# A fused attention and long-convolution kernel: the inverse transform's first stage in pairs, f32 products of q and k in the front, phases two at once, and a new order

## The chip, the core and the metric

The kernel runs on one core of a Trainium2 chip. A core has a matrix engine (PE), a vector engine (DVE), a scalar engine (ACT), a general engine (POOL) and an engine that issues most DMAs (SP). PE reads SBUF and writes PSUM; ACT and DVE read PSUM and write SBUF. Each engine executes its own instructions in the order in which the program lists them, so that an instruction that must wait holds up all that stand behind it on its engine.

The metric is the time of one execution on the device, in microseconds. Times of several executions are told by their median.

## What is computed

Two independent blocks, whose results stand side by side in the output (2048 rows, 576 + 576 columns):

```python
def _A_ref(x, wqkv, wo):               # x: 1 x 2048 x 576, 32 heads of 18, window 256
    q, k, v = ...                       # (x @ wqkv), by heads
    scores = einsum("bhqd,bhkd->bhqk", q, k) * 18 ** -0.5
    scores = where(0 <= i - j < 256, scores, -1e9)
    return (softmax(scores) @ v) @ wo

def _B_ref(u, A, B, C, log_dt, Dskip): # u: 1 x 2048 x 576, 128 states to a channel
    dt = exp(log_dt)
    K = einsum("dn,dnl,dn->dl", C, exp(dt * A * l), dt * B).real
    y = irfft(rfft(pad(u)) * rfft(pad(K)))[:2048]
    return y + u * Dskip
```

Block A is attention in a sliding window of 256 rows. Block B is a convolution of each channel with its own filter K of 2048 taps; K must first be built from 128 complex exponentials to a channel.

## The kernel before

**Stages.** `build` runs four stages in a row, "front", "tables", "first" and "rest". Each stage is a set of streams (generators), and a string in `PLAN` gives the order of their steps by hand: a letter alone is the next step of a stream, a letter with a digit is the oldest piece of later work of that kind (`post`) which a step of this stream has left behind, such as the copy of a product out of PSUM. The instructions are issued in the order of the strings, and each engine takes its own from it. `SLOTS` says which of three PSUM buffers ("ring", two banks each) the next product takes. Two more PSUM buffers ("pp") belong to the projection, later one ("po") to the attention's output.

**Front** (streams A, B: parameters; C: scales; V: v of the first rows; P: projection). x and the weights are loaded. x @ wqkv is made in f16 at the accuracy of f32: each operand is scaled by a power of two and split in a high and a low f16 part, and a product is 14 matmuls (`mm14`, L205: high x high, low x high, high x low over 576 = 4 x 128 + 64 rows, the last rows of both parts put together). The scales need the largest absolute value of all of x and of all weights (`scales`, L193, DVE), taken over the partitions on POOL (L180). `xconv` and `wconv` make the parts. `proj` then makes q and k in nine products of 128 x 512 for each chunk c of 512 rows, and v in eight products of 128 x 288. ACT copies a q/k product as f16 (`qk_hi`, L451), DVE makes the low part (L454), and SP stores both. While the scales aren't known yet, `vfirst` makes v of the first chunk with f32 matmuls from the raw x and weights (L399, L404), eight products of 288 columns.

**Tables** (G, N, R, M, X: the filter K; U: first stage of u's transform; P goes on; Z, s: first steps of the attention). The filter is built in 18 steps q of 32 channels, and half of a step, 16 channels, is c = 2q or 2q + 1. `t_phase` (one for each c) makes phases on PE (512 columns), `fold` takes off their whole turns (an ACT copy to integers at L512, a DVE subtraction at L515), `t_sin` turns them to sines and cosines (ACT, L556 to L558, once for each c), `t_q` multiplies with magnitudes (DVE, L603 to L606), `t_prod` and `t_add` make the other factor (POOL L588, DVE L594), `t_taps` makes 64 matmuls of taps (L617), and `t_dft` the filter's first transform stage. The tile fr, which holds phases and then sines, has FR = 5 buffers of one half each. `s1_u` does the first transform stage of u in 16 steps: it loads ut, multiplies (L494), ACT and DVE copy one half each to ust (L499), and SP stores ust to gx in DRAM. ut and ust have two buffers each (pool s1u).

**Rest** (s, a, v, n: attention; k, c, d, f, e: convolution; l, y, w: output projection). The attention works in 16 items: maxima of scores (L908, L916, DVE L942), scores and exponentials (L984, L997, ACT L1002), products with v (L1022), normalisation. The convolution goes through 24 steps n: `conv_load` loads xk from gx and gk, `spectra` (stream c) makes the second stage of both transforms with 32 matrix products of 64 x 32 tiles (L720, 384 columns) into two ring slots, ACT copies them to X (L728), DVE and POOL multiply the spectra to Y (L736 to L743), and `inverse` (stream d, L754) does the first stage of the inverse transform: 16 matmuls of 32 x 64 tiles over 192 columns. The four groups of 32 rows (b) write to one of the two halves of the PSUM partitions each, 64 (b mod 2), and bank b div 2 of one ring slot. ACT copies the slot to ho (L761), and two DMAs store it to h. `hload` and `clast` do the second stage of the inverse (L817), and `wo` multiplies the attention's output with wo (L205 again).

A matmul of f32 operands shows as two records in the profile.

## Time and profile before

| | us |
|---|---|
| median of the three runs | 777.35 |
| lowest and highest of them | 774.3, 778.51 |
| the profiled execution | 772.85 |
| its span, first to last instruction | 771.1 |

The profile is of one execution. Its page gives the busy time of each engine (PEld is PE's loading of weights, which overlaps with PE), the chain of work that ended last, followed back from the last instruction to what released it, and the costliest groups of instructions by line. In a group's row stand the line, the engine, the operation, what it writes and reads with the shapes, and the count, then the busy time in us and the mean of one in ns, and last the engine's idle time ahead of them with what ended it. In a row of the timeline or the chain the first number is the start and the second the duration, both in us. In a row of the busy times by stage each engine's busy time is followed by its number of instructions. The granted TensorE clock of the whole span is 0.98 of full speed.

| engine | busy us | share of the span |
|---|---|---|
| PE | 686.8 | 89% |
| PEld | 403.5 | 52% |
| DVE | 538.7 | 70% |
| ACT | 548.3 | 71% |
| POOL | 415.8 | 54% |

### The profile page before, as it was taken

To read this page: it belongs to the slowest core of one execution; us is meant where nothing else is said; L and a number is where in the kernel's file an instruction comes from. 1 tells how busy PE (TensorE), PEld (TensorE's weight loads), DVE (VectorE), ACT (ScalarE), POOL (GpSimd) and SP (SyncE) were. 2 spreads that over 40 slices of the span, in tenths; PEclk is the share of its full clock that TensorE was granted. 3 is DMA by queue.
4 is the path that set the end of the run, shared out by engine and by line. 5 is a ranking of instruction groups with operands and counts; after the bars stand their busy time and mean duration, and the time that the engine had idled before them with its cause. 6 is when DMAs were issued, how large, how long until landed. Compare 5 with 4: busy or idle time off the path is not lost.

```text
span 771.1 us, 29480 instructions
## 1 busy us (share of the span) xinstructions
PE 686.8 (89%) x12956; PEld 403.5 (52%) x12956; DVE 538.7 (70%) x689; ACT 548.3 (71%) x755; POOL 415.8 (54%) x309
## 2 busy tenths in 40 slices
PE   3768768999999989999888998989899989999997
PEld 2523334556655655566445545545554545576675
DVE  5884888677787677888859877988886788631200
ACT  2267986888988878895467686677687687766722
POOL 2242886888788696867016553544255355354420
PEclk9978999999999999999989999999999999999999
DMA  8996342863657686757967667586588766767875
GB/s 308 345 248 151 86 109 56 196 156 97 133 146 201 145 195 188 178 150 155 244 213 236 201 186 246 176 273 183 177 246 233 231 206 191 230 189 250 251 237 174
DMA packets 215904, 150.67 MB, mean 195 GB/s; under 512 B 103530, under 2 KB 195818, under 8 KB 215520
## 3 DMA queue, kind: packets, MB, share of 16 engines
q1 hardware_dynamic: 214160, 146.28, 67.0%
q0 software_dynamic: 1616, 2.52, 1.1%
q8 instruction: 101, 1.65, 0.9%
q14 instruction: 27, 0.22, 0.1%
HBM read 83.50 MB, written 65.11 MB: 193 GB/s over the span
## 4 chain that ended last, share of the span: by engine, by line
PE 53%; DVE 12%; ACT 12%; issue 4%; DMA 4%; SPq 2%; POOL 0%; ACTq 0%; DVEq 0%
PE pp L205 9%; PE po L1022 9%; PE ring L205 7%; DVE m L942 5%; PE ring L908 4%; PE ring L754 4%; PE ring L984 4%; PE ring L720 3%; PE ring L617 2%; PE ring L817 2%; PE ring L494 2%; ACT P L1002 2%; PE ring L506 2%; DMA K<-kz 2%; PE ring L633 1%
## 5 line engine op out<-in xcount | busy, mean ns | idle before, releaser
L942 DVE TENSOR_REDUCE m<-ring 128x2 f32<-128x640 f32 (+4 forms) x256 | 188.3, 778 | 42.4 <-PE ring L916 37.1
L588 POOL TENSOR_TENSOR m<-A,tr 128x1024 f32<-128x1024 f32 x72 | 142.0, 1991 | 43.1 <-DVE m L594 37.1
L1002 ACT ACTIVATE P<-ring,esc 128x1024 f32<-128x1024 f32 (+2 forms) x86 | 88.4, 1060 | 28.7 <-PE ring L997 28.0
L1002 ACT ACTIVATE raw<-ring,esc 128x1024 f32<-128x1024 f32 (+2 forms) x74 | 76.9, 1061 | 28.6 <-PE ring L997 26.7
L736 POOL TENSOR_TENSOR t<-X 128x768 f32<-128x768 f32 x24 | 45.9, 1913 | 79.7 <-ACT X L728 79.5
L1065 POOL TENSOR_TENSOR oh<-osb,oh 128x1024 f16<-128x1024 f32 x16 | 35.4, 2211 | 66.2 <-ACT oh L1061 63.3
L205 PE MATMUL pp<-xh,wh 128*128 128x512 f16 x180 | 47.3, 393 | 14.5 <-ACT vst L406 6.4
L205 PEld LDWEIGHTS <-wh 128*128 128x128 f16 x324 | 31.2, 100 | 49.6 <-issue 10.5
L916 PE MATMUL ring<-sm,idb 64*64 64x128 bf16 x896 | 52.8, 219 | 0.0
L603 DVE TENSOR_TENSOR Q<-fr,ring 128x1024 f32<-128x1024 f32 x36 | 43.8, 1216 | 11.6 <-ACT ring L527 11.3
L728 ACT ACTIVATE X<-ring 128x768 f32<-128x768 f32 x48 | 36.7, 811 | 21.2 <-PE ring L720 12.5
L594 DVE TENSOR_TENSOR m<-m,m 128x1024 f32<-128x1024 f32 x36 | 48.3, 1342 | 4.2 <-POOL m L588 4.2
L1057 POOL TENSOR_TENSOR osb<-osb,T 128x1024 f32<-128x1024 f32 x16 | 37.8, 2365 | 24.3 <-DVE T L1052 21.8
L205 PE MATMUL pp<-xh,wl 128*128 128x512 f16 x180 | 48.5, 403 | 1.5 <-DVE wl L373 1.5
L908 PE MATMUL ring<-K,raw 54*64 54x320 f16 (+4 forms) x576 | 43.3, 308 | 5.6 <-DVE m L942 1.6
L569 POOL TENSOR_TENSOR tr<-tr,mab 128x768 f32<-128x768 f32 x18 | 33.7, 1871 | 25.6 <-ACT tr L564 25.6
L908 PEld LDWEIGHTS <-raw 54*64 54x64 f16 x704 | 26.1, 104 | 39.3 <-issue 35.6
L742 POOL TENSOR_TENSOR Y<-t,t 128x384 f32<-128x384 f32 x24 | 24.0, 1000 | 39.7 <-DVE t L736 18.7
L720 PE MATMUL ring<-xk,w 64*32 64x384 f32 x768 | 41.5, 491 | 3.5 <-issue 2.8
L997 PE MATMUL ring<-tm,idb 64*64 64x256 bf16 (+2 forms) x640 | 44.6, 257 | 0.0
L984 PEld LDWEIGHTS <-K 55*64 55x64 f16 x1280 | 29.1, 106 | 27.8 <-issue 24.0
L617 PE MATMUL ring<-Q,m 128*32 128x64 f32 x2304 | 39.2, 220 | 4.1 <-DVE m L594 2.0
(170 smaller groups left out, 1668.5 us busy)
## 6 DMA issues: line engine op xcount, KB each, us to landing
gx<-ust SPq DMA_DIRECT2D x16, 576.0 KB
gk<-kst SPq DMA_DIRECT2D x36, 256.0 KB
xk<-gx SPq DMA_DIRECT2D x24, 384.0 KB
xk<-gk SPq DMA_DIRECT2D x24, 384.0 KB
h<-ho SPq DMA_DIRECT2D x48, 192.0 KB
hp<-h SPq DMA_DIRECT2D x24, 384.0 KB
K<-kz SPq DMA_DIRECT2D x14, 512.0 KB
raw<-qz SPq DMA_DIRECT2D x11, 512.0 KB
```

The lines of the kernel that those rows point to most:

```text
L205: self.nc.tensor.matmul(ps, u, v, start=(i == 0), stop=(i == len(ops) - 1))
L588: tt(m[part], A[:, ch, a0:a0 + 8].unsqueeze(3).to_broadcast(sh), tr[:, ch, part, 0:8].unsqueeze(2).to_broadcast(sh), op=OP.mult)
L594: self.nc.vector.tensor_tensor(m[0], m[0], m[1], op=OP.add)
L617: nc.tensor.matmul(kp[32 * st:32 * st + 32, j, :], m[:, ch, 32 * term:32 * term + 32], Q[:, ch, term, :], start=(term == 0), stop=(term == ...
L720: nc.tensor.matmul(pi[i][32 * b:32 * b + 32, s, :384], self.w2[64 * r:64 * r + 64, t, o:o + 32], x[64 * r:64 * r + 64, 2 * s + q].rearrang ...
L736: mul(ts[i], X[:, :, :, :192].rearrange("p i s j -> p s i j"), X[:, i, :, 192:].unsqueeze(2).to_broadcast(sh), op=OP.mult)
L908: nc.tensor.matmul(ps[z:z + 64, b, :n], d["Q"][rr, 2 * b + pp, 64 * qb:64 * qb + 64], d["K"][rr, 2 * b + pp, k0:k1], start=True, stop=Fals ...
L916: nc.tensor.matmul(out, self.idb[rr], self.sm[rr], start=False, stop=True, skip_group_check=True)
L942: self.nc.vector.tensor_reduce(out, x, axis=AX.X, op=OP.max)
L984: nc.tensor.matmul(ps[z:z + 64, b, off:off + w], d["K"][rr, 2 * b + pp, kc:kc + 64], d["Q"][rr, 2 * b + pp, q0:q0 + w], start=(k == 0), st ...
L1002: nc.scalar.activation(P[:, :, lo:hi], ps[:, :, lo:hi], AF.Exp, scale=self.esc)
L1022: nc.tensor.matmul(po[32 * p:32 * p + 32, z, q0:q0 + w], V[64 * z:64 * z + 64, kb * 76 + 19 * p:kb * 76 + 19 * p + 32], P[p % 2][64 * z:64 ...
```

## The change

There are six parts.

1. `inverse` takes two steps n and n + 1 at once, into two ring slots. Their matmuls alternate, and step n + 1 writes to the other half of the PSUM partitions, so that the four row groups and both halves are in use in turn. The order of the rows in the constant `i1` and the place of `spectra`'s output are exchanged for odd steps, so that Y lies where the second step needs it. There are 12 such pieces.
2. `spectra` is cut in two steps, one ring slot each. X and its products get two buffers (pool fy), Y three (fy2).
3. `t_phase`, `fold` and the sines work on both halves of a step q at once (1024 columns). FR is 3, with buffers of twice the size.
4. In the front, `vfirst` gives way to `qk_first`: q and k products m = 0 to 5 of the first chunk are made with f32 matmuls of 256 columns from raw x and weights, in three ring slots with two products each, and scaled when they are copied out (`qsc`). v of the first chunk is made by `proj` like the others. The weights of v get a scale of their own (`vscale`, with a maximum on ACT), their block is loaded last, and the parts of x and of the weights are made in separate steps, the low ones posted for later.
5. ust has a pool of its own (s1o) with one buffer; ut keeps two.
6. The four strings of `PLAN` and `SLOTS` are new. In "front" there are 13 steps of P ahead of the tables instead of 11 products' thirds and one empty step, in "tables" 27 copies of q/k products instead of 33 and 32 copies of v instead of 24.

The core of the diff:

```diff
-        i1[b ^ s, :, t, s, 0] = np.concatenate([co.T, -si.T], 1)
-        i1[b ^ s, :, t, s, 1] = np.concatenate([si.T, co.T], 1)
+        i1[b ^ s ^ t % 2, :, t, s, 0] = np.concatenate([co.T, -si.T], 1)
+        i1[b ^ s ^ t % 2, :, t, s, 1] = np.concatenate([si.T, co.T], 1)
...
     def inverse(self, n):
-        nc, (ch, t), Y = self.nc, divmod(n, 8), self.Y.pop(n)
-        ps = self.slot()
+        pr = [(k, self.Y.pop(n + k), self.slot()) for k in range(2)]
         for s in range(2):
             for i in range(2):
                 for b in range(4):
-                    o = (2 * s + i) * 64
-                    nc.tensor.matmul(ps[64 * (b % 2):64 * (b % 2) + 64, b // 2, 192 * s:192 * s + 192],
-                                     self.i1[32 * b:32 * b + 32, t, o:o + 64], Y[32 * b:32 * b + 32, i, s],
-                                     start=(s == 0 and i == 0), stop=(i == 1), skip_group_check=True)
+                    for k, Y, ps in pr:
+                        o, z = (2 * s + i) * 64, 64 * (b % 2 ^ k)
+                        self.nc.tensor.matmul(ps[z:z + 64, b // 2, 192 * s:192 * s + 192],
+                                              self.i1[32 * b:32 * b + 32, n % 8 + k, o:o + 64], Y[32 * b:32 * b + 32, i, s],
+                                              start=(s == 0 and i == 0), stop=(i == 1), skip_group_check=True)
+        for k, Y, ps in pr:
+            self.post("1", (ps,), lambda n=n + k, ps=ps: self.h_out(n, ps))
...
-    def spectra(self, n):
+    def spectra(self, n, i):
...
+        for q in range(2):
+            for s in range(2):
+                for r in range(2):
+                    b = 2 * q + (r ^ s ^ n % 2)
...
-    def t_phase(self, c):
-        x = self.slot()[:, 0]
-        self.outer(x, self.ps, c // 2, [self.mul["c_ct"]], c % 2 * HC, HC)
+    def t_phase(self, q):
+        x = self.slot()
+        for e in range(2):
+            self.outer(x[:, e], self.ps, q, [self.mul["c_ct"]], e * HC, HC)
...
-        for c in (2 * q, 2 * q + 1):
-            f = self.fr[c]
-            nc.scalar.activation(f[:, 1], f[:, 0], AF.Abs)
...
+        f = self.fr[q]
+        nc.scalar.activation(f[:, 1], f[:, 0], AF.Abs)
...
+    def qk_first(self):
+        nc, w, x = self.nc, self.wt, self.xt
+        for g in range(NF // 2):
+            ps = None
+            for h in range(2):
+                cs = slice(256 * g + 128 * h, 256 * g + 128 * h + 128)
+                for hf in range(2):
+                    yield "PE", (w, x[hf]), *(("ring",) if ps is None else ())
+                    self.hold = ps = self.slot() if ps is None else ps
+                    for k in range(4):
+                        nc.tensor.matmul(ps[:, h, 256 * hf:256 * hf + 256], w[:, k, cs], x[hf][:, k], start=(k + hf == 0),
+                                         stop=False, skip_group_check=True)
             yield "PE", ()
             for hf in range(2):
+                for h in range(2):
+                    r, cs = slice(64 * h, 64 * h + 64), slice(256 * g + 128 * h, 256 * g + 128 * h + 128)
+                    nc.tensor.matmul(ps[:, h, 256 * hf:256 * hf + 256], w[r, 4, cs], x[hf][r, 4], start=False, stop=True,
+                                     skip_group_check=True)
...
+    def vscale(self):
+        nc, sp = self.nc, self.p["const"]
+        yield "Activation", (self.wt,)
+        nc.scalar.activation(self.wl[:, :, 1152:1728], self.wt[:, :, 1152:1728], AF.Abs, accum_out=self.amx[:, 10:11])
...
-            st = self.p["s1u"].tile([128, 2, D], F32, name="ust")
+            st = self.p["s1o"].tile([128, 2, D], F32, name="ust")
...
-        w(2)
+        w(0)
         x(0)
         x(1)
-        w(0)
         w(1)
         for c in range(2, 8):
             x(c)
+        w(2)
...
-            self.FR = 5
+            self.FR = 3
...
-            for n, b in (("cc", 1), ("fs", 2), ("fy", 1), ("wo", 1), ("wo2", 1), ("wor", 2), ("wy", 2)):
+            for n, b in (("cc", 1), ("fs", 2), ("fy2", 3), ("fy", 2), ("wo", 1), ("wo2", 1), ("wor", 2), ("wy", 2)):
```

The part of the new order of "tables" that holds steps 1 and 2 of u's transform (U is a step, U1 and U2 are the two copies to ust, U4 is its store):

```
U4UUP4U1U2U4P1PP2RXX5X
```

More of the change, by code (lines that the diff above doesn't have):

```diff
@@ L28 @@
 NQ = 18
+NF = 6
 GC = 4 * JJ
@@ L144 @@
+    "201210212020"
 )
@@ L401, in vfirst @@
             yield "PE", ()
             for hf in range(2):
-                r = slice(64 * hf, 64 * hf + 64)
-                nc.tensor.matmul(ps[hf], x[r, 4, ts], w[r, 4, 1152 + 288 * hf:1440 + 288 * hf], start=False, stop=True)
-            for hf in range(2):
-                self.post("1", (ps[hf],), lambda v=v, hf=hf, x=ps[hf]: nc.scalar.activation(
-                    v[:, 16 * hf:16 * hf + 16, 0:18], x.rearrange("p (h d) -> p h d", d=18), AF.Copy))
-        yield "SP", (), lambda: self.known and not self.pend.get("V1")
@@ L429, in proj @@
                 self.post("1", (ps,), lambda c=c, m=m, ps=ps: self.qk_hi(c, m, ps))
-            for tk in range(4 if c else 0):
+            for tk in range(4):
                 v = self.vst[tk]
@@ L495, in s1_u, with store @@
                                      ut[ch][64 * r:64 * r + 64, 288 * k:288 * k + 288], start=True, stop=True)
-            end = self.both("4", (st,), lambda ch=ch, st=st: nc.sync.dma_start(gv[:, ch:32:16], st))
+            def store(ch=ch, st=st):
+                nc.sync.dma_start(gv[:, ch:32:16], st)
+                self.n["u"] += 1
+            end = self.both("4", (st,), store)
             def evac(op, r, st=st, ps=ps, end=end):
@@ L723, in spectra @@
         sh = [128, 2, 2, 192]
         def first():
-            X = fy.tile([128, 2, 2, 384], F32, name="X")
-            for i in range(2):
-                nc.scalar.activation(X[:, i], pi[i][:, :, :384], AF.Copy)
-            ts = [None, None]
-            end = self.each(lambda: self.post("3", (), lambda: third(*ts)))
-            self.post("2", (X,), lambda: second(X, 0, tt, ts, end))
-            self.post("6", (X,), lambda: second(X, 1, nc.gpsimd.tensor_tensor, ts, end))
+            if i == 0:
+                self.X[n] = fy.tile([128, 2, 2, 384], F32, name="X")
@@ L734, in second @@
+            X = self.X[n]
+            nc.scalar.activation(X[:, i], pi[:, :, :384], AF.Copy)
+            if i:
+                del self.X[n]
+                ts = [None, None]
+                end = self.each(lambda: self.post("3", (), lambda: third(*ts)))
+                self.post("2", (X,), lambda: second(X, 0, tt, ts, end))
+                self.post("6", (X,), lambda: second(X, 1, nc.gpsimd.tensor_tensor, ts, end))
         def second(X, i, mul, ts, end):
@@ L784, in cspec @@
     def cspec(self):
-        self.spd = set()
+        self.X = {}
         for n in range(24):
-            yield "PE", lambda: (self.cl[n],), "ring", "ring", lambda: n in self.cl and self.n["Y"] >= n
-            self.spectra(n)
-            self.spd.add(n)
+            for i in range(2):
+                yield "PE", lambda: (self.cl[n],), "ring", lambda: n in self.cl and self.n["Y"] >= n
+                self.spectra(n, i)
     def cinv(self):
-        for n in range(24):
-            yield "PE", lambda: (self.Y[n],), "ring", lambda: n in self.Y
+        for n in range(0, 24, 2):
+            yield "PE", lambda: (self.Y[n], self.Y[n + 1]), "ring", "ring", lambda: n + 1 in self.Y
             self.inverse(n)
@@ L851, in early @@
                 part()
+            self.loaded = i + 1
     def item(self, i):
@@ L873, in load @@
             part()
+        self.loaded = i + 1
     def parts(self, i):
@@ L1039, in aload @@
                 part()
+            self.loaded = i + 1
     def norm(self):
```

277 lines of the change are left out of this document (135 added, 142 removed).

## The prediction

> **What bounds it now.** I read the page's busy shares and chain first, then the busy times by stage, then the chain and the groups inside each stage.
>
> ```profile
> span 771.1 us, 29480 instructions
> ...
> PE 686.8 (89%) x12956; PEld 403.5 (52%) x12956; DVE 538.7 (70%) x689; ACT 548.3 (71%) x755; POOL 415.8 (54%) x309
> ...
> PE 53%; DVE 12%; ACT 12%; issue 4%; DMA 4%; SPq 2%; POOL 0%; ACTq 0%; DVEq 0%
> PE pp L205 9%; PE po L1022 9%; PE ring L205 7%; DVE m L942 5%; PE ring L908 4%; PE ring L754 4%; PE ring L984 4%; PE ring L720 3%; PE ring L617 2%; PE ring L817 2%; PE ring L494 2%; ACT P L1002 2%; PE ring L506 2%; DMA K<-kz 2%; PE ring L633 1%
> ```
> ```profile
> core 0: us, PE busy (x) PEld busy (x) DVE busy (x) ACT busy (x) POOL busy (x), PEclk, DMA share, GB/s
> ...
> 60.00:365.00 305.00, 277.15 (x3925) 160.61 (x3924) 231.17 (x297) 255.45 (x430) 233.52 (x183) 0.98 0.60 146
> ...
> 370.00:670.00 300.00, 273.24 (x7328) 151.73 (x7324) 240.97 (x319) 212.56 (x231) 127.97 (x84) 0.99 0.71 215
> 670.00:771.00 101.00, 96.64 (x1473) 67.83 (x1465) 16.81 (x18) 53.88 (x63) 37.03 (x21) 1.00 0.73 223
> ```
> The reader is to see three stages. In the tables (60 to 365) four engines are loaded alike: ACT is busy 84% of it, POOL 77%, DVE 76%, PE 91% (PE's figure holds the drains of its matmuls). No one engine bounds it; ACT has the least slack of the three others. From 370 on PE is busy 91%, after 670 96%, and PE is over half of the chain; work taken from PE there comes off the end nearly one for one. The front, up to about 60, is this:
>
> ```profile
> 12.50 6.94 PE L399 MATMUL pp<-wraw,raw 128*128 128x288 f32 x16 [12.50 <-DMA raw<-in_xr_dram]
> ...
> 20.61 4.15 PE L399 MATMUL pp<-wraw,raw 128*128 128x288 f32 x16 [0.49 <-ACT vst L406]
> ...
> 23.29 3.14 DVE L193 TENSOR_REDUCE amx<-wraw 128x1 f32<-128x2880 f32 x1
> 24.69 0.76 PE L404 MATMUL pp<-wraw,raw 64*128 64x288 f32 x4
> ...
> 37.97 0.15 DVE L189 TENSOR_SCALAR xr<-xr 128x1 f32<-128x1 f32 x1
> 38.15 2.61 ACT L383 ACTIVATE xh<-raw,xr 128x1280 f16<-128x1280 f32 x2 [3.67 <-DVE xr L189]
> 42.49 2.29 PE L205 MATMUL pp<-xh,wh 128*128 128x512 f16 x5 [6.39 <-ACT vst L406]
> 59.42 0.33 PE L506 MATMUL ring<-c_ca,Tre 96*128 96x384 bf16 x1
> ```
> PE multiplies v in f32 until 36.1, stands idle 6.4 us until the scale of x (38.1) has made xh, and reaches the first table product at 59.4.
>
> **The inverse in pairs.** A step of L754 is 16 f32 matmuls (32 records, two passes each).
>
> ```profile
> 477.04 1.46 PE ring L754 x32
> ...
> 584.24 2.76 PE ring L754 x64
> ...
> 655.20 1.44 PE ring L817 x8
> ...
> 678.25 1.45 PE ring L720 x32
> ```
> ```profile
> L754 PE MATMUL ring<-Y,i 32*64 32x192 f32 x768 | 36.1, 326 | 1.0 <-DVE m L942 0.5 <-ACT P L1002 0.2
> ```
> One step takes 1.46, two in a row 2.76: 1.30 of streaming and 0.16 of drain. L817 fills two tiles at a time (128 rows, 64 columns): 8 records of 384 columns in 1.44, so (1.44 - 0.16) / 4 = 0.32 for a round of 384 columns, 0.16 for 192. L754's 32 records in 1.30 are then 8 rounds of four tiles: half the array. L720 (64*32) puts 32 records of 384 columns in 1.45, four rounds of eight: the array does run eight tiles with eight different streams. So I take 8 rounds of eight for a pair: 1.30 + 0.16 = 1.46. Twelve pairs save 12 x (2.76 - 1.46) = 15.6, or 12 x 1.46 = 17.5 where the steps now stand apart. 24 spectra become 48 halves of the same 32 records; in the new order's string nine steps have other PE work between their halves, 9 x 0.16 = 1.4 more drain. Net -14.2 to -16.1: I take **-15** and keep 0 and -17.5 as ends.
>
> ```profile
> L761 ACT ACTIVATE ho<-ring 128x768 f32<-128x768 f32 x24 | 19.4, 811 | 13.2 <-PE ring L754 10.4 <-DMA hp<-h 2.1 <-DMA ol<-od 0.5
> ```
> A pair holds two of the three ring slots till ACT has made two copies of 0.81; spectra did so 24 times and do it no more. The pair's four h stores follow each other on SP instead of two and two; the 48 stores stay. Between -10 (12 x 0.81) and +10 on PE, taken as 0.
>
> The Trainium skill's page TensorE: Matmul & The Clock Gate (the passage "Wait — 56ns, not 53.3ns?" in Part 1) says that matmuls never start closer than about 25 ns. By it a pair's 64 records need 1.60 + 0.16, and the sum would lose 12 x 0.30 = 3.6. The trace disagrees:
>
> ```profile
> 182.71 1.10 PE ring L617 x64
> ```
> 64 records in 1.10 are 17 ns apart, so no such floor enters.
>
> **Phases two at once.**
>
> ```profile
> L527 ACT ACTIVATE ring<-ring 128x1024 f32<-128x1024 f32 x36 | 36.1, 1015 | 5.5 <-PE ring L506 5.3
> L603 DVE TENSOR_TENSOR Q<-fr,ring 128x1024 f32<-128x1024 f32 x36 | 43.8, 1216 | 11.6 <-ACT ring L527 11.3
> L558 ACT ACTIVATE fr<-fr,halfpi 128x512 f32<-128x512 f32 x36 | 25.4, 706 | 0.0
> L515 DVE TENSOR_TENSOR fr<-ring,fr 128x512 f32<-128x512 f32 x36 | 24.1, 683 | 5.1 <-ACT fr L512 5.1
> L557 ACT ACTIVATE fr<-fr 128x512 f32<-128x512 f32 x36 | 22.7, 630 | 0.9
> L556 ACT ACTIVATE fr<-fr 128x512 f32<-128x512 f32 x36 | 22.5, 625 | 0.3 <-DVE fr L515 0.3
> L512 ACT ACTIVATE fr<-ring 128x512 int32<-128x512 f32 x36 | 21.0, 599 | 5.6 <-PE ring L506 5.0 <-DVE Q L606 0.6
> ```
> Doubling the width on ACT adds 1015 - 599 = 416 ns, so an instruction of 512 carries about 0.18 of fixed cost. Four kinds lose 18 instructions each: 72 x 0.18 = 13.0 off ACT. DVE: 18 x (2 x 0.683 - 1.216) = 2.7. PE's products stay. fr has 3 double buffers for 5 single ones, but a double one is free only after both its Q's; I put nothing on that. ACT is not alone in the stage, so I take **-8** of the 13 (ends 0 and -13): what is late next is POOL or PE.
>
> **Front.** f32 v leaves: 4 x (4.15 + 0.76) = 19.6 on PE. f32 q and k come: 48 full matmuls of 256 columns, (4.15 / 8) x 256 / 288 = 0.46 each, 22.1, and 12 of half the rows in pairs, 6 x 0.76 x 256 / 288 = 4.1: 26.2, in three ring slots that nothing else wants yet.
>
> ```profile
> 285.95 3.02 PE pp L205 x14
> ...
> 351.29 1.82 PE pp L205 x14
> ```
> ```profile
> 38.63 8.76 SPq L472 DMA_DIRECT2D vd<-vst  x8
> ...
> 39.41 0.51 POOL L309 DMA_DIRECT2D Tre<-splre  x1
> ```
> Six f16 products of 14 matmuls go (6 x 3.02 = 18.1), eight of v come (8 x 1.82 = 14.6): 3.5 less behind the scales, 6.6 more ahead of them, where 6.4 was idle. The third weight block is loaded last and its 3.14 of maximum leaves DVE ahead of the scale of x: 38.1 becomes about 35. Against that ACT and DVE get six copies and six low parts, and ACT the maximum of v's weights (2880 columns at xh's 2.61 / 2560: 2.9), between the scale and the second half of xh: 6 x 0.60 + 2.9 = 6.5 on ACT by the copies' row above. v's burst of eight stores, 8.76 of SP, falls away and goes out two by two later, so q's and k's first stores meet a free queue. POOL's load of Tre now stands behind the all-reduce of v's maximum, some 40 by the last block's landing near 35 and these 2.9; it needs 5.6 to land (row below), before 55. In the tables 27 q/k copies stand for 33 and 32 v copies for 24: nothing. I see the first f16 product near 42 as before and the first table product at 55 to 63: **-2**, ends -5 and +4.
>
> **One buffer for ust.** The copy of a step must wait until the store of the step before has landed.
>
> ```profile
> gx<-ust SPq DMA_DIRECT2D x16, 576.0 KB
> ...
> splre<-hre POOLq DMA_DIRECT2D x3, 144.0 KB, 9.0
> ...
> Tre<-splre POOLq DMA_DIRECT2D x1, 432.0 KB, 5.6
> ```
> Its landing isn't shown; the rows bound it by 5.6 and 9.0. Behind a waiting copy stand all of ACT's (or DVE's) next instructions, and two of the three ring slots stay taken. Summing the rows' durations along the new order's string, five of the 15 copies follow the store before with less than 2.5 us of work between; the others have 4 to 20. Uncovered cost 5 x (9.0 - 1.5) = 37 at most, 0 at least. Nearest is 5.6, 5 x 4.1 = 20 of waiting; ACT alone has 305 - 255 = 50 idle in the stage to absorb it: I take **+3**.
>
> xk, X and t get more buffers, wl's low parts go out later: nothing, their consumers are PE-bound.
>
> **Sum**: -15 - 8 - 2 + 3 = -22. The profiled execution took 772.85 (span 771.1); it goes to about 751. The median of the three runs shown is 777.35, 4.5 above it, so I forecast 777.35 - 22 = 755.
>
> **Rivals.**
> *A, the pair is no faster than two steps.* In the piece two row tiles write each PSUM bank at a time, in opposite halves of the partitions. If they had to take turns, a pair would stay at 2.76, and -15 would be +1: 777.35 - 22 + 16 = 771. Against it: the 32 records in 1.46 already have two row tiles on one bank. (The Trainium skill, TensorEngine Tiling (Array Packing), Gotcha 1: PSUM Pressure, says that different row tiles cannot use the same bank at once; by that rule one step would take 16 rounds and read 2.76, so the trace disagrees for opposite halves.) What remains for A is four rows by two columns together, which no row shows. Chance 0.14.
> *B, slower: the ust wait.* Place: the five copies above. Price: 5 x 7.5 = 37 if the store takes 9.0 and nothing covers it: 777.35 - 25 + 37 = 790. It eats the whole gain of 25 from 5 us a place on, a landing of 6.5. For it: two ring slots are held meanwhile. Against: ACT's 50 idle, and that the ten other places are covered. Chance 0.12.
> *C, ACT's saving is lost in the tables* because POOL and PE are close behind, and the front is not earlier: 777.35 - 15 + 3 = 765. Chance 0.16.
>
> **Numbers.** Forecast 755, chance 0.58, its own range 743 to 764. The ends of all terms give 742 (-17.5 - 13 - 5) and above 790. The range 741 to 771 holds the forecast, C and half of A, 0.8. A measurement tells about 0.5% from no change, 773.5 to 781. Faster: 0.56 of the forecast, 0.14 of C, 0.09 of A, 0.01 of B, 0.80. Same: 0.09. Slower: 0.11.
>
> **What would show it.** The piece's 64 records in 1.4 to 1.6 on the chain and its group at 18 us busy instead of 36.1 (2.7 a pair: A). Eighteen phase instructions of each kind at 1.03 to 1.13, ACT 13 less busy. The x scale near 35, table products from 55 to 63. Copies of ust waiting for a DMA by over 3 us in several places: B. Tables that end less than 5 us earlier though ACT is less busy: C. The forecast is wrong above all if the piece halves PE's work and PE then waits for ring slots instead.

## The result and the profile after

| | before | after |
|---|---|---|
| median of 20 runs | 776.3 us (771.0 to 782.1) | 780.3 us (776.2 to 787.5) |
| ratio | 1 | 1.0059, 95% interval 1.0032 to 1.0085 |
| profiled execution, span | 771.1 us | 780.5 us |

By the ratio the change is 4.6 us slower, by little but clearly; the prediction said 22 us faster. Ratios, here and below, are of the executions within 1.5% of the fastest of their kernel, so a ratio and the medians of all executions can differ (most for after_max_half, where three of ten lie outside). The two profiled executions lie 9.4 us apart, about twice as much, because that of before is one of the fastest of its kernel. So differences between stages below are good to some 5 us, and the verdicts rest on the ratios.

From the page of the changed kernel, the span, the busy times and the chain of work that ended last:

```profile
span 780.5 us, 29553 instructions
...
PE 681.7 (87%) x13024; PEld 408.2 (52%) x13024; DVE 544.8 (70%) x676; ACT 547.7 (70%) x689; POOL 419.4 (54%) x310
...
PE 39%; DVE 10%; ACT 8%; DMA 5%; issue 4%; POOL 2%; SPq 2%; ACTq 0%; DVEq 0%; POOLq 0%
```

PE's work fell by 5 us in all, and the end did not follow. PE's 39% here and the 53% before can't be compared as they stand: the shares are of the whole span, and this chain is followed back only to 229 us, that of before to 96. In the last stage alone the chain's pieces on PE add up to about 239 us, 262 before. The groups of instructions (line, engine, operation, tiles, count, then busy us and mean ns of one, then idle time before them) that the two large terms of the sum were about:

```profile
L776 PE MATMUL ring<-Y,i 32*64 32x192 f32 x768 | 21.6, 337 | 0.2 <-ACT raw L1027 0.2
...
L579 ACT ACTIVATE fr<-fr,halfpi 128x1024 f32<-128x1024 f32 x18 | 20.4, 1133 | 0.0
L577 ACT ACTIVATE fr<-fr 128x1024 f32<-128x1024 f32 x18 | 19.1, 1064 | 0.0
L578 ACT ACTIVATE fr<-fr 128x1024 f32<-128x1024 f32 x18 | 19.0, 1057 | 0.2
L533 ACT ACTIVATE fr<-ring 128x1024 int32<-128x1024 f32 x18 | 18.4, 1022 | 0.6 <-PE ring L527 0.6
```

Both mechanisms work. The inverse's products take 21.6 us of PE instead of 36.1, and the four kinds of phase instructions are down to eighteen of 1.02 to 1.13 us.

PE's, ACT's and the others' busy times in the tables, for the same window as in the prediction:

```profile
60.00:365.00 305.00, 271.61 (x3817) 162.64 (x3819) 238.61 (x281) 249.03 (x360) 236.57 (x183) 0.95 0.62 146
```

ACT is busy 6.4 us less there (249.0 for 255.5), PE 5.5, and yet the stage takes longer; the granted clock is 0.95 for 0.98.

The stages, by the instructions of one line (shortest, median and longest in ns, then the first and the last start). The spectra of the tables, before and after, then the first table product of after:

```profile
L633 PE MATMUL ring<-Kq,wk x288: 374/374/521, 101.2 to 370.0; 32*128 32x256 f32 x144
```
```profile
L654 PE MATMUL ring<-Kq,wk x288: 374/374/787, 98.9 to 377.4; 32*128 32x256 f32 x144
...
L527 PE MATMUL ring<-c_ca,Tre x18: 322/328/527, 61.8 to 323.3; 96*128 96x384 bf16 x18
```

The first table product went from 59.4 to 61.8 (+2.4), the tables' last product from 370.0 to 377.4 (so +5.0 in the tables), and the last stage from 401.1 to 403.1 us (+2.0). No stage became shorter. Five other profiles have the front and the tables of before (before_half, before_max_half, before_both, rest_new and pair_old2, all below). In them the first table product starts between 60.0 and 62.0 and the tables end between 370.6 and 374.0. So the later end of the tables is clear of the spread; the later first product is hardly.

What became of PE's work in the last stage is in the busy times of a window (us, then PE, PEld, DVE, ACT, POOL busy with counts, the granted clock, the DMA share, GB/s), first before, then after:

```profile
370.00:775.00 405.00, 369.88 (x8793) 219.56 (x8785) 257.79 (x337) 266.44 (x293) 164.99 (x104) 0.99 0.71 215
```
```profile
378.00:785.00 407.00, 358.68 (x8725) 209.86 (x8724) 253.53 (x329) 266.79 (x294) 168.30 (x104) 0.97 0.70 213
```

PE is busy 11.2 us less, though the inverse alone gave 14.5: the rest runs at a lower granted clock (0.97 for 0.99). And it stands idle 780.5 - 378 - 358.7 = 43.8 us instead of 771.1 - 370 - 369.9 = 31.2. The saving became waiting.

The profile names what ended most of that idle time. Summed over PE's waits in the last stage, those for VectorE's maxima go from 8.1 to 9.4 us, those for ScalarE from 7.5 to 10.8, those for DMAs from 2.5 to 5.2, and those for which it shows no releaser ("issue") from 6.8 to 12.0. Some of the rows (who waited, for whom, us in total, times, longest), before and after:

```profile
PE ring L908 <- DVE m L942: 3.6, 13, 0.4
PE ring L720 <- issue: 2.8, 4, 1.1
```
```profile
PE ring L933 <- DVE m L967: 7.4, 21, 1.2
PE ring L1009 <- issue: 5.2, 3, 2.5
PE ring L941 <- issue: 2.5, 1, 2.5
```

### The profile page after: what moved, and what is told of

Read it like the earlier page. It is cut to its first block, busy times and chain, and to the rows that moved or that the text cites. A ratio compares the mean times of both kernels' runs of the same rounds, so it can differ in the third digit from the quotient of the medians.

```text
span 780.5 us, 29553 instructions
## 1 busy us (share of the span) xinstructions
PE 681.7 (87%) x13024; PEld 408.2 (52%) x13024; DVE 544.8 (70%) x676; ACT 547.7 (70%) x689; POOL 419.4 (54%) x310
## 4 chain that ended last, share of the span: by engine, by line
PE 39%; DVE 10%; ACT 8%; DMA 5%; issue 4%; POOL 2%; SPq 2%; ACTq 0%; DVEq 0%; POOLq 0%
PE po L1047 8%; PE ring L206 6%; DVE m L967 6%; PE ring L933 4%; PE ring L739 4%; PE ring L1009 4%; PE pp L206 3%; PE ring L841 2%; PE ring L776 2%; ACT raw L1027 2%; PE ring L1022 1%; PE ring L638 1%; POOL m L609 1%; DMA gx<-ust 1%; PE ring L527 1%
## 5 line engine op out<-in xcount | busy, mean ns | idle before, releaser
L1027 ACT ACTIVATE raw<-ring,esc 128x1024 f32<-128x1024 f32 (+2 forms) x74 | 76.7, 1061 | 31.2 <-PE ring L1022 30.8
L615 DVE TENSOR_TENSOR m<-m,m 128x1024 f32<-128x1024 f32 x36 | 56.2, 1561 | 9.2 <-POOL m L609 9.1
L933 PE MATMUL ring<-K,raw 54*64 54x320 f16 (+4 forms) x576 | 45.9, 317 | 11.7 <-DVE m L967 5.3
L624 DVE TENSOR_TENSOR Q<-fr,ring 128x1024 f32<-128x1024 f32 x36 | 43.8, 1216 | 11.0 <-ACT ring L548 10.8
L748 ACT ACTIVATE X<-ring 128x768 f32<-128x768 f32 x48 | 36.9, 813 | 17.3 <-PE ring L739 14.5
L206 PE MATMUL pp<-xh,wh 128*128 128x512 f16 x150 | 40.7, 401 | 9.2 <-DVE xh L400 5.2
L1022 PE MATMUL ring<-tm,idb 64*64 64x256 bf16 (+2 forms) x640 | 46.6, 262 | 1.8 <-issue 1.8
L1009 PEld LDWEIGHTS <-K 55*64 55x64 f16 x1280 | 30.9, 109 | 31.1 <-issue 27.3
L638 PEld LDWEIGHTS ring<-Q,m 128*32 128x32 f32 x2304 | 34.7, 111 | 21.4 <-issue 8.7
L764 POOL TENSOR_TENSOR Y<-t,t 128x384 f32<-128x384 f32 x24 | 27.1, 1129 | 34.4 <-DVE t L758 34.0
L206 PEld LDWEIGHTS <-wh 128*128 128x128 f16 x270 | 25.4, 101 | 36.9 <-issue 12.4
L548 ACT ACTIVATE ring<-ring 128x1024 f32<-128x1024 f32 x36 | 36.3, 1014 | 10.5 <-PE ring L527 10.0
```

Of the source, the lines that this page charges most:

```text
L206: self.nc.tensor.matmul(ps, u, v, start=(i == 0), stop=(i == len(ops) - 1))
L615: self.nc.vector.tensor_tensor(m[0], m[0], m[1], op=OP.add)
L638: nc.tensor.matmul(kp[32 * st:32 * st + 32, j, :], m[:, ch, 32 * term:32 * term + 32], Q[:, ch, term, :], start=(term == 0), stop=(term == ...
L933: nc.tensor.matmul(ps[z:z + 64, b, :n], d["Q"][rr, 2 * b + pp, 64 * qb:64 * qb + 64], d["K"][rr, 2 * b + pp, k0:k1], start=True, stop=Fals ...
L1009: nc.tensor.matmul(ps[z:z + 64, b, off:off + w], d["K"][rr, 2 * b + pp, kc:kc + 64], d["Q"][rr, 2 * b + pp, q0:q0 + w], start=(k == 0), st ...
L1022: nc.tensor.matmul(out, self.idb[rr], self.tm[rr, 64 * at:64 * at + n * w], start=False, stop=True, skip_group_check=True)
```

## The experiments

All ratios are to the kernel before. 1% is 7.8 us.

### Is it the pair? The loop moved, and the pair in the old order

**after_seq**: the changed kernel with one loop moved outwards.

```diff
-        for s in range(2):
-            for i in range(2):
-                for b in range(4):
-                    for k, Y, ps in pr:
+        for k, Y, ps in pr:
+            for s in range(2):
+                for i in range(2):
+                    for b in range(4):
```

> The changed kernel with one loop moved: the 16 products of the first step of each pair are issued before the 16 of the second, so that only half of the array tiles take products at a time; all else as changed. Theory PACE: the piece goes from about 1.6 back to about 3 us, 12 pieces, and all of it comes off the end: 1.019 to 1.028 of before, that is 10 to 17 us over the changed kernel at 1.006. Theory SLOTS, or any theory in which something other than TensorE sets the end of the changed kernel's last stage: at most 4 us over the changed kernel, 1.004 to 1.011 of before.

Measured 780.2 us, ratio 1.0048 (1.0019 to 1.0077), beside the changed kernel's 1.0059. The group of its inverse products:

```profile
L776 PE MATMUL ring<-Y,i 32*64 32x192 f32 x768 | 30.0, 355 | 0.3 <-ACT raw L1027 0.3
```

With 8.4 us of PE put back nothing is lost, so keeping all eight tiles busy is worth nothing at the end of this kernel. SLOTS as it was worded isn't shown by that; PACE has fallen for the changed order.

**pair_old**: before's order with the pair in place of every second step, Y in three buffers, and each ring slot given to the step for whom it had been free longest in the written order. **pair_old2**: the same instructions in the same order, other digits in `SLOTS`:

```diff
 SLOTS = (
-    "0121201201201220120212012010210012012012102102121012102012012020021021012010120102102001201200010221"
+    "0121201201201202122012012010120020120102102121010201200120120102102102120122102102100221021022210221"
...
```

> The kernel before with the pair of inverse steps alone: front, tables, phases, U buffers and order as before, each second step of the inverse now does the work of two (both slots, one copy each behind it, Y in three buffers of their own). Theory PACE (TensorE sets the pace of the last stage, the pair's saving is real, and the change's new order gave it back): the pieces' line falls from about 36 to about 22 us, the idle time of TensorE in the rest stays near 31 us, the time is 0.980 to 0.990 of before (8 to 15 us less). Theory SLOTS (a step that holds two ring slots at once costs what it saves, whatever the order): TensorE's idle time in the rest grows by 10 us or more, with waits for the copies out of the slots, and the time is 0.997 to 1.005 of before.

> The pair of inverse steps alone once more, in the order of before; all that differs from pair_old is which of the three ring slots each step gets. In pair_old every slot was the one whose copy stands longest ago in the written order; here front, tables and first keep the slots of before, and in the last stage each step gets the slot whose reader ended earliest in the trace of before. Theory SLOT CHOICE (the 66 us of pair_old are waits for a wrongly chosen slot, not a price of the pair): at most 1.01 of before, and the tables end near 370 us as before. Within it, PACE (TensorE's work in the last stage comes off the end one for one): 0.980 to 0.990. SLACK (TensorE's saving turns into idle time of TensorE, as moving the loop in the changed kernel did, 0.1 us for 8.4 us of products): 0.994 to 1.006.

pair_old took 843.4 us, 1.085 (1.0817 to 1.0882); pair_old2 795.1 us, 1.0225 (1.018 to 1.0269). **Which slot a step gets is worth 48 us** of the 66, and it shows in the tables already, where pair_old changes nothing else: they end at 397.9 us, in pair_old2 at 374.0. PE's waits there in pair_old (us in total, times, longest):

```profile
PE ring L506 <- DVE Q L606: 13.8, 6, 8.6
PE ring L633 <- DVE Q L606: 5.8, 5, 1.6
```

PE is in order, so a step that waits for the one slot which VectorE still reads holds up everything behind it, even if another slot is free. pair_old therefore says nothing of the pair. pair_old2 says more: its last stage takes 419.5 us for 401.1, and it is 18 us slower than before. Its slots there were chosen by one trace of before, so how much of the 18 us is the pair and how much still the digits was not separated. Part of it shows in PE's waits of the last stage:

```profile
PE ring L720 <- DMA xk<-gk: 4.2, 2, 4.0
PE ring L910 <- ACT ho L764: 4.1, 9, 0.6
```

(In the profile before, L908 waited 0.9 us for ho.) A pair wants two slots at once and posts two copies behind each other; dropped into an order that was not made for it, it cost more than it saved with both sets of digits. No theory of pair_old2 named so much (SLOT CHOICE said 1.01 at most): the miss is ours.

**new_old** and **new_old2** put the old last stage's order, with pairs, behind the changed tables, again with the two ways to choose slots.

> The changed kernel (its front, phases, single U buffer, tables and pair as they are) with its last stage's order put back to that of before, pairs in place of every second inverse step and the two halves of each spectra step side by side; ring slots are given out least recently used. Theory ORDER (the changed order of the last stage gave the pair's saving back): the last stage is 8 us or more shorter than the changed kernel's 375 us, 0.985 to 0.998 of before. Theory FRONT-AND-TABLES (what was lost was lost before the last stage, and by the clock after it): the last stage is as long as in the changed kernel, within 4 us, 1.002 to 1.010 of before. An order that was drawn up for other tables may wait at its start for spectra that come at other times: a wait for q, k or the spectra of over 5 us near 400 us would make this run say nothing.

> The changed kernel with the last stage's order of before (pairs for every second inverse step, the two halves of a spectra step next to each other), slots chosen by the release times in the trace of before. Theory ORDER (the changed order of the last stage costs something): last stage 8 us or more shorter than the changed kernel's 402.7 us, 0.985 to 0.998 of before. Theory FRONT-AND-TABLES: last stage within 4 us of the changed kernel's, 1.002 to 1.010 of before. The order was drawn up for spectra and scores that come at other times, so a run over 1.01 would say only that an order does not carry over.

824.7 us, 1.0622 (1.0588 to 1.0655), and 791.8 us, 1.0176 (1.0122 to 1.023). The slots again are worth 33 us. ORDER and FRONT-AND-TABLES both missed. As the expectation says of a run over 1.01, this shows only that the old order does not carry over; what the changed order costs has to come from the next run.

**rest_new** is the converse, the changed last stage on before's front and tables.

> The kernel before in its front, tables and first stage (phases one at a time, two U buffers, three-product q and k), with the last stage of the changed kernel: pairs, halves of a spectra step in slots of their own, and the changed order, slots chosen by the release times in the changed kernel's trace. If the changed kernel's loss lies in front and tables (they end 7.5 us later in its trace, its last stage 1.9 us longer), this run is 0.995 to 1.004 of before. If the last stage alone is what makes it slower, 1.004 to 1.010. If pair and order do pay once the tables end early: 0.985 to 0.994, and this version would beat both.

773.6 us, ratio 0.9971 (0.9945 to 0.9996). This is all that the pair, the split spectra and their order are worth: **2 us**. In the profile the last stage is no shorter for it (402.0 us, 401.1 before), so these 2 us have no place yet. The run fits the first of its three theories: it is a little faster than both kernels, and 7 us faster than the changed one, whose loss lies, as far as the parts add up, in the front and the tables.

### What is a saving on one engine worth?

These leave work out of the kernel before and touch neither order nor slots. **before_half** and **before_max_half**, then both:

```diff
-            for i in range(2):
+            for i in range(1):
...
-                                     start=(s == 0 and i == 0), stop=(i == 1), skip_group_check=True)
+                                     start=(s == 0), stop=True, skip_group_check=True)
```
```diff
-                self.post("2", (ps,), lambda out=mv[:, :, 8 * pp + qb], x=ps[:, :, :n]: self.red(out, x))
+                self.post("2", (ps,), lambda out=mv[:, :, 8 * pp + qb], x=ps[:, :, :n // 2]: self.red(out, x))
```

> The kernel before, order and slots untouched, with the second half of the products of each inverse step left out (the i=1 products: 16 of 32 in each of 24 steps; the inverse transform's output is then a partial sum). This takes about 24 x 0.77 = 18 us off TensorE in the last stage, more than the pair can, and changes nothing else. Theory PACE: all of it, or nearly, comes off the end: 14 to 19 us less, 0.975 to 0.983 of before. Theory SLACK: the time goes into TensorE's waits (maxima on VectorE, copies on ScalarE, DMAs) and a slower granted clock after them: 0 to 6 us less, 0.992 to 1.000.

> The kernel before with each of its 256 maxima taken over the first half of its columns (the other half of each score row is left out of the maximum): VectorE loses about 234 x 0.37 = 86 us of work in the last stage, and each of these steps gives its ring slot back 0.37 us earlier; TensorE's work is as before. Theory PACE (TensorE sets the end of the last stage): at most 8 us less (the 8.1 us in which TensorE waits for maxima). Theory SLOTS (the end hangs on how long the three slots are held: fill, wait and copy, shared by TensorE, VectorE and ScalarE): 86 us over three slots is 29 us, 15 to 29 us less, 0.962 to 0.981.

> The kernel before with both cuts of the last stage at once: half of the inverse's products left out (alone: TensorE 15 us less, 5 us off the end) and each maximum over half of its columns (alone: VectorE 65 us less in the last stage, 4 to 6 us off the end). Theory ADDITIVE (each engine's work has its own small share in the end): 8 to 12 us less, 0.984 to 0.990. Theory PARALLEL (TensorE's queue and the slots' readers are each almost the longest chain, so that a cut in one is stopped by the other): 14 us or more less, 0.982 or under. Theory ORDER-BOUND (the written order and its transfers set the end, and any cut gives the same few us): 4 to 7 us less, 0.991 to 0.995.

772.2 us, 0.9927 (0.9892 to 0.9963); 771.6 us, 0.9936 (0.9905 to 0.9966); 765.4 us, 0.9862 (0.9814 to 0.9911). The last stage of before_half, then of before_max_half:

```profile
370.00:775.00 405.00, 358.64 (x8417) 206.67 (x8417) 260.35 (x338) 265.78 (x293) 165.08 (x104) 0.97 0.70 215
```
```profile
370.00:775.00 405.00, 368.71 (x8801) 221.13 (x8801) 192.83 (x338) 266.01 (x293) 165.07 (x104) 0.98 0.70 214
```

In before_half the products' group falls from 36.1 to 20.6 us, by 15.5. In the profiles 4 of these come back, with a clock of 0.97 for 0.99 (PE's busy time falls by 11.2 only), 9 turn into idle time (768.9 - 370 - 358.6 = 40.3 for 31.2), and 2 come off the span; by the runs it is 5, as the profile of before is a fast one. PE's waits for the maxima grow from 8.1 to 13.2 us, those for ScalarE from 7.5 to 11.2. VectorE's 65 us less give 5 as well. PACE has fallen with the products, of which it wanted 14 to 19 us (its "at most 8" for the maxima holds), and so has SLOTS, which wanted 15 to 29 from the maxima. The two cuts together give 11, so they add up, as far as four executions tell (7 to 14). Neither PE nor VectorE paces this stage alone; ScalarE and GpSimd were not cut there.

The same in the tables. **before_third** leaves out the third product of q, k and v, **before_nosin** one sine of each phase, **before_poolhalf** half of GpSimd's second table product:

```diff
-        ops = [(wh, xh, k) for k in range(5)] + [(wl, xh, k) for k in range(5)] + [(wh, xl, k) for k in range(4)]
+        ops = [(wh, xh, k) for k in range(5)] + [(wl, xh, k) for k in range(5)] + ([(wh, xl, k) for k in range(4)] if part is None else [])
```
```diff
-            nc.scalar.activation(f[:, 0], f[:, 0], AF.Sin, scale=-TWO_PI)
```
```diff
+            k = 4 if part else 8
-            tt(m[part], A[:, ch, a0:a0 + 8].unsqueeze(3).to_broadcast(sh),
+            tt(m[part][:, :, 0:k], A[:, ch, a0:a0 + k].unsqueeze(3).to_broadcast([128, HC, k, 8]),
```

> The kernel before with the third of the three products of q, k and v (low part of x by high part of w, 4 of 14 matmuls, chunks 1 to 3) left out: some 40 us less on TensorE in the tables (132 x 0.22 + 96 x 0.12), order, slots and the other engines as before. Theory TENSORE-PACES-TABLES (it is 91% busy there): 28 to 40 us less, 0.949 to 0.964. Theory SHARED (the slots, the order and the copies of all engines pace them together, so that one engine's work comes off at a fraction): 8 to 22 us less, 0.972 to 0.990.

> The kernel before with the first of the two sines of each phase left out (36 instructions of 0.63 us on ScalarE, 22.7 us of the tables; the sine rows of the table then hold the phase itself). Order, slots, TensorE, VectorE as before. Theory ACT-IN-TABLES (the prediction's: 13 us off ScalarE are worth 8 of the end): 10 to 17 us less, 0.978 to 0.987. Theory TABLES-PACED-ELSEWHERE: at most 5 us less, 0.993 to 1.000.

> The kernel before with the second of GpSimd's two table products over half of its rows (36 x about 1.0 us less on GpSimd in the tables; VectorE's sum adds that half twice). The tables gave 0 for 33 us of TensorE and 3 for 22.7 us of ScalarE. Theory GPSIMD-LOOP (the tables go at the pace of the loop product - sum - taps - next product, with GpSimd's two products in it): 15 us or more less, 0.981 or under. Theory ORDER-BOUND: at most 5 us less, 0.993 to 1.000.

777.9 us, 1.0045 (1.0006 to 1.0083); 773.4 us, 0.9961 (0.9937 to 0.9985); 778.6 us, 1.001 (0.9979 to 1.0041). The stage of 60 to 370 us in the three, in this order:

```profile
60.00:370.00 310.00, 253.78 (x3795) 146.71 (x3793) 236.00 (x300) 259.59 (x434) 234.59 (x183) 0.93 0.59 146
```
```profile
60.00:370.00 310.00, 282.12 (x4098) 165.35 (x4097) 239.80 (x305) 243.27 (x400) 236.27 (x183) 0.98 0.61 149
```
```profile
60.00:370.00 310.00, 279.03 (x4044) 163.52 (x4045) 231.26 (x301) 259.32 (x434) 200.01 (x183) 0.99 0.61 149
```

In the profile of before this window has 280.3 of PE, 259.6 of ACT and 233.5 of POOL. Taking 27 us from PE gives nothing (the clock falls to 0.93), 16 from ACT give 3 at the end, 34 from POOL nothing. GPSIMD-LOOP, ACT-IN-TABLES and TENSORE-PACES-TABLES have fallen (and SHARED for PE, which wanted 8 to 22): none of the three engines paces the tables alone. That the written order with its hand-overs (slot, copy, next engine, buffer) sets their length is what is left, and argued, not shown: which hand-overs these are was not isolated, and VectorE's table work was not cut.

### The phases two at once

**after_split** undoes the instructions' width in the changed kernel and nothing else:

```diff
-        nc.scalar.activation(f[:, 1], f[:, 0], AF.Abs)
+        for h in range(2):
+            nc.scalar.activation(f[:, 1, h], f[:, 0, h], AF.Abs)
```

(and so for the copy, both sines and VectorE's subtraction).

> The changed kernel with its phases still two at once in slots, tiles and order, but each of the four ScalarE instructions and the one VectorE subtraction over 128 x 1024 issued as two over 128 x 512: ScalarE gets its 13 us of the tables back (72 x 0.18), VectorE 2.7. Theory ACT-IN-TABLES (the prediction's: ScalarE has least slack there, so its saving was worth about 8 us): 5 to 13 us over the changed kernel, 1.012 to 1.022 of before. Theory TABLES-PACED-ELSEWHERE (TensorE with its drains, and the waits of the chain, set the tables' end): at most 3 us over the changed kernel, 1.002 to 1.010.

783.9 us, 1.0087 (1.0051 to 1.0123): 2 us over the changed kernel's 1.0059, and the intervals overlap. That is under the bound of ACT-IN-TABLES. The split puts only 7.7 us back on ACT's busy time (555.4 for 547.7), not 13; these are worth about 2, if anything.

**phase_old3** is before with the phases alone at once, **rest_phase3** the same with the changed last stage. Both need 4 KB that two smaller buffers free; **before_pools** has only those:

```diff
-("fap", 2), ("trp", 3)
+("fap", 2), ("trp", 2)
...
-        t1 = self.p["tab1"].tile([128, GC, 2, 4], F32, name="t1")
+        t1 = mab.rearrange("p c m -> p (c m)")[:, 0:8 * GC].rearrange("p (c i m) -> p c i m", i=2, m=4)
```

> Control for the next two: the kernel before with two buffers instead of three for the factors' sines (tr) and one scratch tile of GpSimd laid over the exponentials' tile that is just used up, so that 4 KB a partition come free. If these buffers cost nothing, 0.997 to 1.003 of before; if ScalarE now waits for tr, up to 1.01.

> The kernel before with the phases two at once alone (the place of the second of each two in the order, slots as before), two U buffers kept by means of the smaller buffers of the control. ScalarE loses 13 us and VectorE 2.7 us in the tables; the order of all else is that of before. Theory ACT-IN-TABLES (the prediction's): 5 to 13 us less than the control, 0.983 to 0.994 of it. Theory SHARED (an engine's work comes off at a small fraction, as 22.7 us of sines left out gave 3): 0 to 4 us less, 0.995 to 1.000. A loss of over 2 us would say that holding one slot for two phases costs more than the instructions save.

> All of the change but its front, its single U buffer and its order of the tables: before's front and tables with the phases two at once (as in phase_old3), and the changed last stage with its pairs (as in rest_new, 0.997 of before). Theory FRONT-AND-TABLE-ORDER (what made the changed kernel slower, 1.006, is its front, the single U buffer and the new order of its tables): 0.990 to 0.998 of before, 6 us or more under the changed kernel. Theory PHASES (holding the slot longer for two phases makes the tables later): the loss is here already, 1.001 to 1.008.

Control 787.8 us, 1.0162 (1.0116 to 1.0208), more than it was given: one buffer of tr less and GpSimd's scratch tile laid over mab (the exponentials' tile) cost 13 us together, while 34 us of GpSimd's work cost nothing. They were not run apart, but the trace speaks for the scratch. It has a wait of ScalarE that the profile before hasn't, for mab, which now comes free only when A is made; ScalarE's first instruction on tr has no idle time ahead of it:

```profile
ACT mab L547 <- POOL A L579: 6.7, 3, 2.9
```

phase_old3 793.2 us, 1.0234 (1.0195 to 1.0272), 5.5 us over its control, with intervals that overlap; rest_phase3 785.5 us, 1.0123 (1.0072 to 1.0173), which is 0.999 of control times rest_new. Its two theories, which left out what the control costs, both missed. So the phases at once are worth between nothing and a loss of some 5 us, depending on the order about them. Groups of phase_old3 show where a loss can come from:

```profile
L555 ACT ACTIVATE fr<-fr 128x1024 f32<-128x1024 f32 x18 | 19.1, 1062 | 6.7 <-DVE fr L514 6.7
...
L511 ACT ACTIVATE fr<-ring 128x1024 int32<-128x1024 f32 x18 | 18.4, 1024 | 8.6 <-PE ring L505 8.5
```

Before, ACT waited 0.3 us for fr at this place and 5.0 for PE: the first half's subtraction ran while ACT copied the second. With one wide piece ACT waits for VectorE each time it has nothing else in its order. The changed kernel's own order covers this (0.0 in its row of L577 above), so there it is not the loss.

### The maxima in the tables' tail

The changed order draws maxima forward. VectorE's maxima between 340 and 370 us, before and after:

```profile
L942 DVE TENSOR_REDUCE m<-ring 128x2 f32<-128x640 f32 (+4 forms) x22 | 12.0, 590 | 2.5 <-PE ring L919 2.0 <-PE ring L916 0.4
```
```profile
L967 DVE TENSOR_REDUCE m<-ring 128x2 f32<-128x640 f32 (+4 forms) x27 | 15.3, 621 | 0.9 <-PE ring L944 0.8
```

**after_max_half** is the cut of before_max_half made in the changed kernel.

> The changed kernel with each of its 256 maxima over the first half of its columns (the other half of each score row is left out of the maximum). In the kernel before the same cut gave 5 us. Theory MAXIMA-BURSTS (the changed order puts runs of maxima where VectorE then holds up the tables' end and the slots: 27 maxima, 15.3 us, between 340 and 370 us against 22, 12.0): 10 us or more off the changed kernel's 1.006, 0.993 of before or under. Theory NO-OTHER-THAN-BEFORE: 3 to 7 us off it, 0.996 to 1.002.

774.9 us, 0.9935 (0.9902 to 0.9967): 9.6 us under the changed kernel by the ratios, 5.4 by the medians of all executions, where the same cut gave 5 before. The spectra of its tables end 3.5 us earlier, where in the kernel before that cut did not bring the tables' end forward:

```profile
L654 PE MATMUL ring<-Kq,wk x288: 374/374/791, 99.2 to 373.9; 32*128 32x256 f32 x144
```

So, by one pair of profiles, about half of the 7.4 us by which the tables end later goes with VectorE's work in their tail. But of the 13.7 us between these two profiles 10.2 lie in the last stage (392.9 us for 403.1), which MAXIMA-BURSTS doesn't single out. Its bound of 10 us was missed narrowly, and by the medians the gain lies in the other theory's 3 to 7: the run does not decide between them.

## Why the prediction was wrong

**The step that failed is in "What bounds it now": "work taken from PE there comes off the end nearly one for one."** It was read from PE's 91% busy share and from its majority in the chain. before_half took 15.5 us of PE out of exactly that stage and got 5; after_seq put 8.4 back and lost none. A chain names what came last, not what stands next. In the last stage of before no wait of PE for VectorE's maxima or for ScalarE is longer than 0.5 us: these engines are that close behind. So the 15 us became waits (24.9 us of them before, 37.4 after) and slower products at a lower clock (0.97 for 0.99). The prediction's last sentence on what would make it wrong ("the piece halves PE's work and PE then waits for ring slots instead") is the case, though slots are only a part of it: copies, transfers and spells without a releaser grew more than the waits for maxima.

**The pair, -15.** The piece was right: 64 records in 1.56 to 2.3 us for 1.46, 21.6 us in all for 18. Only the longest, at 550.5 us, lies in a stretch of half clock; why others take up to 2.1 was not traced. At the end the pair with its order is worth -2 (rest_new). **Slots held, 0 (-10 to +10).** In before's order +18 with the saving already in it (pair_old2), some of it perhaps the digits', so beyond its end; in an order made for it, it is in the -2. **Phases, -8 (0 to -13).** The four kinds lost 14.7 us in their rows (91.6 to 76.9), though ACT's total stayed at 547.7 for 548.3: the new order loads function tables 33 times for 29, 1.28 us each, the maximum of v's weights takes 2.8, and the rest was not traced. Even so the term was wrong by its premise, not by that: ACT's time there is worth about a fifth (3.0 for 16.3 in before_nosin; 2.2 for 7.7 in after_split, within the noise). "ACT has the least slack" was a busy share, and shares of 84, 77 and 91% did not tell that ACT, POOL and PE would each give next to nothing. Rival C had the right sign for this.

**Front, -2 (-5 to +4).** The scale of x came at 36.5 for "about 35", PE's f32 took 24.4 + 3.4 = 27.8 us for 26.2, and the first table product came at 61.8, inside 55 to 63 but 2.4 later than before. Half of that stands ahead of the first f16 product, 43.7 for 42.5: it waits for the second half of xh, which ACT makes behind copies of the f32 products and the maximum of v's weights. Like before's first five (2.29 us in the prediction's lines), it runs at half clock:

```profile
43.67 2.41 PE L206 MATMUL pp<-xh,wh 128*128 128x512 f16 x5 [2.59 <-ACT xh L393]
```

The same five take 1.24 at full clock (a row in the last section). As before's had this too, the half clock is not what made the front later; the estimate used full-clock rows for both.

**One ust buffer, +3 (0 to +37), and rival B.** No copy of ust waited for the store before it by more than this:

```profile
  PE ring L512: 13.6, 12
  DMA gx<-ust: 0.2, 1
```

B is out as a mechanism; the new order keeps the steps of U apart (its products start for the last time at 350.8 instead of 334.4). **Rival A** is out: the eight tiles do run together (21.6 us of products, 30.0 with the loop moved).

What remains open: the 7 us between rest_new and the changed kernel lie in the front (at most 2.4 by the traces) and the tables. How they fall to the maxima of the tail, the single ust buffer, the order about it and the phases was not separated by a run.

## What to carry to other kernels

In a kernel whose order has already been balanced by hand, a busy share of 91% or a chain that is half PE doesn't give the worth of a saving; leave out work on that engine, at unchanged order, and see how much the end moves, before building the real thing (here 15.5 us gave 5, 27 gave 0, 34 gave 0). Predict with the exchange rate found. Give coarser pieces (two slots at once, wider hand-overs) a price of their own: pair_old2 and phase_old3 came out slower for all the work they saved, though neither isolates that price. And with a fixed order, the assignment of buffers is part of the schedule: digits alone were worth 48 us.

## What the runs showed of the hardware that was not expected

**A wait of PE is paid twice.** The changed kernel's PE, round one wait in the tables, and the granted clock in the windows ahead, over and behind:

```profile
203.91 1.04 PE L206 MATMUL pp<-xh,wh 128*128 128x512 f16 x4
208.15 0.58 PE L206 MATMUL pp<-xh,wh 128*128 128x512 f16 x1 [3.20 <-DVE xh L400]
208.53 2.34 PE L206 MATMUL pp<-xh,wl 128*128 128x512 f16 x5
...
214.31 1.24 PE L206 MATMUL pp<-xh,wl 128*128 128x512 f16 x5
```
```profile
200.00:207.30 7.30, 4.45 (x147) 3.21 (x137) 7.27 (x5) 7.27 (x12) 6.34 (x6) 1.00 0.65 136
207.30:214.10 6.80, 5.95 (x15) 2.04 (x15) 3.85 (x6) 4.55 (x7) 3.49 (x5) 0.50 0.73 137
214.10:220.00 5.90, 5.90 (x31) 2.75 (x30) 2.79 (x4) 2.33 (x4) 4.76 (x4) 1.00 0.28 77
```

After 3.2 us without work the clock is at 0.50 for 6.8 us, and five products take 2.34 instead of 1.24. The half clock begins 2.4 us into the idle spell. In all traces here the recorded clock changes only in steps of 3.41 us, so that half clock lasts 3.4, 6.8, 10.2 or 13.7 us at a time; in all it is 61 us of the changed kernel's span and 31 of before's. The Trainium skill's page TensorE: Matmul & The Clock Gate (HAM oscillation — how this bites in real kernels) says that the clock drops after an idle gap of more than about 3.4 us; the halving is as it says, but here a gap of 3.2 was enough, and one of 2.59 in the front's row above. The profiles of kernels with PE work taken out show a lower mean clock: 0.980 before, 0.968 in before_half, 0.958 in before_third, 0.961 after the change (over executions 0.971 to 0.985 before, 0.959 to 0.978 in before_half). That the clock caused a part of the loss was not tested by a run of its own.

**PE stands still for nothing that the profile names.** The last stage of the changed kernel has four such spells of over 1.2 us, 8.7 us in all, that of before one of 1.4. One of the four:

```profile
547.32 0.30 PE L1009 MATMUL ring<-Q,K 55*64 55x256 f16 x2 [2.45 <-issue]
```

In these two traces and seven others there are 30 such spells in the last stage, and each ends 2.2 to 2.6 us after the start of a 16 KB transfer on the instruction queue, of which there are some hundred in a run. That PE waits for its own instructions there suggests itself; no run tested it. rest_new, which has the pairs too, has one such spell (1.4 us), so the pairs alone don't bring them.

**Small buffers can outweigh an engine.** The two space savings of before_pools cost 13 us, with hardly an instruction added (29481 for 29480).
